# Loading the first input blocks of a blocked convolution by 121 lanes and by pairs of 50 lanes in place of 128

## The chip, the cores and the metric

The kernel runs on one core of one Trainium2 chip. The metric is the time of one execution on the device, in microseconds (us), as the median of several runs. TensorE (PE) multiplies matrices, VectorE (DVE), ScalarE (ACT) and GpSimd (POOL) do element-wise work, and the queue of SyncE (SP) issues the transfers, which run on the core's 16 DMA engines. A lane is one of the 128 partitions of the on-chip memory.

## The reference

Two steps: a long convolution along the sequence by FFT, and then a small expert layer on the 128 best-scored positions of each batch.

```python
# x: (8, 6336, 128), h: (6336, 128), float32
Xf = np.fft.rfft(x, n=2*S, axis=1); Hf = np.fft.rfft(h, n=2*S, axis=0)
y = np.fft.irfft(Xf * Hf[None], n=2*S, axis=1)[:, :S]
scores = y @ w_gate
for b in range(B):
    top = np.argpartition(-scores[b], 128)[:128]
    ye = np.maximum(y[b, top] @ w1, 0) @ w2
    y[b, top] += 1 / (1 + np.exp(-scores[b, top]))[:, None] * ye
```

## The kernel before

The transforms are written as products with tables of sines and cosines. The work is cut into units: unit -1 is the filter `h`, units 0 to 7 are the data. Each unit has eight input blocks. Block n belongs to unit n // 8 - 1, so blocks 0 to 7 are the filter, 8 to 15 are unit 0, and 16 onwards the later units. A block is a 128 x 1024 array of float32 in memory, 512 KB. On the host, 50 rows are put in lanes 0 to 49 and 50 rows in lanes 64 to 113; the other 28 lanes are zeros.

Stage A takes one block at a time. `load_x(n)` puts it into one of nine slots of the buffer `half`. `fold(n, v)` makes two passes of VectorE over it, a sum (L133) and a difference (L134). `products_a` then makes 2 x 16 TensorE products (L195, t = 0 and 1) with the lanes b*64 to b*64 + 49 alone, from the table `fah` for the filter and from `fa` for all data units, and `leave_a` copies them out of the accumulator by ScalarE (L212) and, from the fourth block of unit 0 on, in part by VectorE (L210). There are three accumulator places in turn.

The order is written out by hand in `plan`: stage A of unit -1, then stage A of unit 0, then steps "j", which join the filter's spectrum (`stage_h`, whose products stand at the helper's line L109) and unit 0's middle stage; then the stages of later units, interleaved. Blocks 0 to 8 are loaded ahead of all work. After the second half of block b of unit -1 (b = 0 to 6), the load of block b + 9 is issued on SP, into the slot that block b leaves. After block 3, behind the load of block 12, stand the loads of the constants `cst` and of the table `fa` (L848, L849). The folds are put on VectorE four blocks ahead of the products: ahead of the products of block b stands the fold of block b + 4, and the copies out of block b come behind it.

Each transfer that SP issues counts on one of eight semaphores in turn (DMAHW0 to DMAHW7 below), so a transfer waits until the one eight places ahead of it has landed.

Of the kernel before, what the change touches and what calls it, by code (L numbers as in the profile page):

```python
# [18 lines left out]
N1, N2 = 50, 128  # L19
# [5 lines left out]
LN = 114  # L25
# [8 lines left out]
def conv_moe(ctx, tc, x, h, w_gate, w1, w2, fa_d, wb_d, wc_d, at_d, tri_d, cst_d, outs):  # L34
    nc = tc.nc
# [75 lines left out]
    blocks = {}  # L111

    def place(n):
        u, q = n // 8 - 1, n % 8
        if u >= 2 and 0 < q < 5:
            o = 6400 + 1600 * (0, 1, 3, 2)[q - 1]
            return reg[u % 2][:, o:o + 1536]
        i = 10 + max(0, q - 4) % 3 if u >= 2 else (n + 3) % 9 if n < 16 else n - 13
        return half[:, i * 1536:i * 1536 + 1536] if i < 10 else xr[i - 10]

    def load_x(n):
        u, q = n // 8 - 1, n % 8
        t = place(n)
        for i in range(2 if n == 0 else 1):
            w = slice(i * 512, i * 512 + 512) if n == 0 else slice(0, 1024)
            nc.sync.dma_start(out=t[:, w], in_=h[q, :, w] if u < 0 else x[u, q])
        blocks[n] = (t[:, 0:1024].rearrange("p (d s m) -> p d s m", d=8, s=2),
                     t[:, 1024:1536].rearrange("p (d m) -> p d m", d=8))

    def fold(n, eng):  # L130
        for i in range(2 if n == 0 else 1):
            xs, es = [a[:, i * 4:i * 4 + 4] if n == 0 else a for a in blocks[n]]
            eng.tensor_tensor(out=es, in0=xs[:, :, 0], in1=xs[:, :, 1], op=ALU.add)  # L133
            eng.tensor_tensor(out=xs[:, :, 0], in0=xs[:, :, 0], in1=xs[:, :, 1], op=ALU.subtract)  # L134

# [608 lines left out]
    for u in range(NU):  # L744
        if u + 2 <= NU:
            both = merge(c_list(u), b_list(u + 1))
            n = next(i for i, s in enumerate(both) if s[0] == "b") + 2 * (u % 2)
# [56 lines left out]
    for n in range(9):  # L804
        load_x(n)
    v.memset(ones16, 1.0)
    v.memset(edges[:, 0:1], -1.0)
    v.memset(edges[:, 1:2], -0.5)
    fold(0, v)
    done = [1]  # L810

    def fold_to(n):
        while done[0] <= min(n, 23):
            fold(done[0], v if done[0] < 16 or done[0] in (20, 21, 23) else g)
            done[0] += 1
# [10 lines left out]
    for s in plan:  # L826
        kind, unit = s[0], s[1]
        n = (unit + 1) * 8
# [5 lines left out]
        if kind == "a":  # L834
            q, t = s[2:]
            if unit < 2 and t == 0:
                fold_to(min(n + q + 4, 15) if unit < 1 else 23)
            if unit >= 2 and (q, t) == (3, 0):
                fold(n + 7, g)
# [5 lines left out]
            if t and n + q < 7:  # L845
                load_x(n + q + 9)
# [5 lines left out]
            if unit >= 2 and (q, t) == (1, 0):  # L852
                load_x(n + 7)
            if t:
                visit("pqx" if q and q % 2 == 0 else "x")
        elif kind == "j":
# [4 lines left out]
            n = KCH[c][1] * HD  # L861
# [23 lines left out]
        elif kind == "c":  # L885
            stage_c(*s[1:])
            i = HALVES.index(s[2] // 2 * 2)
            free = True
            if unit + 2 < NU and s[2] % 2:
# [4 lines left out]
                q = (None, 0, None, None, 1, 4, 2, (3, 5))[i] if last else (None, 0, 5, 6, 1, 4, 2, 3)[i]  # L894
# [21 lines left out]
        elif kind == "d":  # L916
            busy[0] = unit + 1 == NU
            stage_d(*s[1:], tabs.pop(s))
            i = s[2]
# [129 lines left out]
```

## Time and profile before

| | |
|---|---|
| median of 3 runs | 785.18 us (784.46 to 789.2) |
| the profiled execution | 789.5 us, with a span of 787.7 us from first to last instruction |
| PE busy | 728.6 us, 92% of the span |
| DVE, ACT, POOL busy | 631.2, 449.4, 550.0 us |
| DMA | 157.64 MB, mean 200 GB/s |
| mean granted PE clock | 0.991 of full |

The page gives each engine's busy time, then the span in 40 slices of some 20 us. The change lies in the first two slices: stage A of the filter and of unit 0 runs from the start to 42.7 us. The profiled execution is 4.3 us longer than the median, and its span 1.8 us shorter than its own time.

### The profile page before, as it was taken

How to read it: one execution, taken by the hardware profiler on the slowest of the kernel's cores; microseconds unless marked ns; L12 is line 12 of the kernel's file. 1: busy time of each engine (PE TensorE's matmuls, PEld its weight loads, DVE VectorE, ACT ScalarE, POOL GpSimd, SP SyncE). 2: the span in 40 equal slices, each digit the busy share in tenths (PEclk: the TensorE clock that was granted, in tenths of full speed). 3: DMA queues.
4: the chain of work that ended last, by engine and by line, in shares of the span. 5: the costliest groups of instructions: out<-in, count | busy, mean ns of one | idle time of the engine just before them, and what ended most of it. 6: DMA issues, size and time to landing. Idle time of an engine off the chain costs nothing.

```text
span 787.7 us, 39722 instructions
## 1 busy us (share of the span) xinstructions
PE 728.6 (92%) x17566; PEld 630.3 (80%) x17566; DVE 631.2 (80%) x1072; ACT 449.4 (57%) x962; POOL 550.0 (70%) x405
## 2 busy tenths in 40 slices
PE   6899889999999999999999999999999998878665
PEld 5777678888889879888898789888897888868554
DVE  6579967767676799899777999999688998975983
ACT  5687643465346556656366466555564666665562
POOL 0029929976997599759968697877895756623733
PEclk9899999999999999999999999999999999999989
DMA  8539637567856775678557765699569736460500
GB/s 329 194 133 333 242 113 243 174 198 235 272 186 196 243 267 181 179 240 274 176 168 231 254 218 146 189 363 303 152 211 298 242 107 179 131 197 20 156 15 17
DMA packets 82292, 157.64 MB, mean 200 GB/s; under 512 B 9366, under 2 KB 30088, under 8 KB 82120
## 3 DMA queue, kind: packets, MB, share of 16 engines
q1 hardware_dynamic: 81224, 154.05, 61.0%
q8 instruction: 138, 2.26, 1.2%
q0 software_dynamic: 896, 1.05, 0.5%
q14 instruction: 34, 0.28, 0.1%
HBM read 121.77 MB, written 33.29 MB: 197 GB/s over the span
## 4 chain that ended last, share of the span: by engine, by line
PE 66%; DVE 17%; issue 5%; DMA 4%; POOL 3%; ACT 2%; SPq 1%; another core or an unknown queue 0%; POOLq 0%; DVEq 0%; ACTq 0%
PE pb L301 24%; PE pt L109 18%; PE pt L195 10%; PE pb L321 10%; DVE cmp L472 2%; DVE ss L353 2%; PE pb L195 2%; DVE tx L283 2%; PE pb L109 1%; POOL big L288 1%; DMA out<-st 1%; PE pm L109 1%; DVE st L330 1%; ACT junk L485 1%; DVE st L331 1%
## 5 line engine op out<-in xcount | busy, mean ns | idle before, releaser
L302 ACT COPY half<-pb 114x512 f32<-114x512 f32 x224 | 147.0, 656 | 166.8 <-PE pb L301 166.3
L288 POOL TENSOR_TENSOR big<-big,tx 128x512 f32<-128x512 f32 (+1 forms) x104 | 132.0, 1303 | 70.3 <-DVE tx L283 60.8
L337 POOL TENSOR_TENSOR tm<-st,wg 114x1024 f32<-114x1024 f32 x56 | 133.9, 2394 | 59.9 <-DVE st L331 41.3
L288 POOL TENSOR_TENSOR reg<-reg,tx 128x512 f32<-128x512 f32 (+1 forms) x104 | 130.8, 1291 | 44.3 <-PE pb L301 22.6
L301 PE MATMUL pb<-wc,reg 128*50 128x64 f32 x4096 | 125.6, 219 | 4.4 <-issue 3.7
L301 PEld LDWEIGHTS pb<-wc,reg 128*50 128x50 f32 x4096 | 120.4, 126 | 8.4 <-issue 5.2
L301 PEld LDWEIGHTS pb<-wc,big 128*50 128x50 f32 x4096 | 118.5, 126 | 4.1 <-issue 1.1
L301 PE MATMUL pb<-wc,big 128*50 128x64 f32 x4096 | 121.0, 219 | 0.8 <-issue 0.8
L321 PE MATMUL pb<-half,wbuf 114*50 114x128 f32 x1792 | 110.9, 273 | 2.9 <-issue 1.5
L321 PEld LDWEIGHTS pb<-half,wbuf 114*50 114x50 f32 x1792 | 96.5, 122 | 9.6 <-issue 2.5
L109 PE MATMUL pt<-big,wbuf 128*64 128x256 f32 x704 | 86.4, 388 | 0.5 <-issue 0.5
L109 PE MATMUL pt<-reg,wbuf 128*64 128x256 f32 x704 | 85.0, 388 | 0.0
L212 ACT COPY reg<-pt 128x800 f32<-128x800 f32 x66 | 58.0, 932 | 38.7 <-PE pt L195 37.2
L283 DVE TENSOR_TENSOR tx<-pt,wbuf 128x1024 f32<-128x1024 f32 (+1 forms) x65 | 76.3, 1174 | 0.0
L330 DVE TENSOR_TENSOR st<-pb,st 114x512 f32<-114x512 f32 x56 | 38.6, 689 | 42.1 <-PE pb L321 27.1
L109 PEld LDWEIGHTS pt<-big,wbuf 128*64 128x64 f32 x704 | 52.1, 135 | 23.7 <-issue 1.0
L109 PEld LDWEIGHTS pt<-reg,wbuf 128*64 128x64 f32 x704 | 51.7, 135 | 21.4
L355 DVE TENSOR_REDUCE ss<-tm 114x16 f32<-114x1024 f32 x48 | 58.4, 1216 | 7.5 <-POOL tm L337 6.9
L212 ACT COPY big<-pt 128x800 f32<-128x800 f32 x56 | 49.2, 938 | 24.3 <-PE pt L195 24.3
L283 DVE TENSOR_TENSOR reg<-pt,wbuf 128x1024 f32<-128x1024 f32 (+1 forms) x39 | 45.9, 1178 | 17.9 <-PE pt L109 17.8
L195 PE MATMUL pt<-fa,big 50*64 50x100 f32 x2336 | 59.2, 249 | 0.3 <-issue 0.3
L195 PEld LDWEIGHTS pt<-fa,big 50*64 50x64 f32 x2336 | 51.9, 133 | 6.5 <-issue 3.6
(177 smaller groups left out, 1193.8 us busy)
## 6 DMA issues: line engine op xcount, KB each, us to landing
wbuf<-tab_at SPq DMA_DIRECT2D x112, 200.0 KB
out<-st SPq DMA_DIRECT2D x112, 200.0 KB
wbuf<-tab_wb SPq DMA_DIRECT2D x84, 256.0 KB
wbuf<-hd SPq DMA_DIRECT2D x84, 256.0 KB
big<-in_x SPq DMA_DIRECT2D x37, 512.0 KB
half<-in_x SPq DMA_DIRECT2D x15, 512.0 KB
hd<-st SPq DMA_DIRECT2D x24, 256.0 KB
reg<-in_x SPq DMA_DIRECT2D x12, 512.0 KB
```

The source lines that it names most:

```text
L109: nc.tensor.matmul(out[lo:hi], w[:, lo:hi], r, **k)
L195: nc.tensor.matmul(o, w, tab[lanes, c], start=True, stop=True)
L212: nc.scalar.copy(out=o, in_=i)
L283: v.tensor_tensor(out=dst.rearrange("p h a j k t -> p k h a j t"), in0=src, in1=w, op=ALU.mult)
L288: g.tensor_tensor(out=yv[:, :, r], in0=yv[:, :, r], in1=zv[:, :, 1 - r], op=ALU.add if r else ALU.subtract)
L301: nc.tensor.matmul(pt[i2 * 64:i2 * 64 + N1, o:o + HD], w, wc[:, i2], start=True, stop=True)
L302: nc.scalar.copy(out=hv[0:LN, c * 4 + j:c * 4 + j + 2].rearrange("p j r m t -> p (j r) t m"), in_=pt[0:LN].rearrange("p (j t m) -> p j t m ...
L321: nc.tensor.matmul(pt[r][a * 64:a * 64 + N1, c * 128:c * 128 + 128], ats[c // 2][0:LN, c % 2, a, r], hv[0:LN, :, r, m], start=True, stop=True)
L330: v.tensor_tensor(out=st[:, 0:512], in0=pt[1][0:LN], in1=st[:, 512:1024], op=ALU.add)
L337: (v if split else g).tensor_tensor(out=tm.rearrange("p (a d) -> p a d", d=n), in0=st.rearrange("p (a d) -> p a d", d=n), in1=w.unsqueeze( ...
L353: v.tensor_reduce(out=ss[u][:, 0, :, 4 * i + k:4 * i + 4], in_=tv[:, :, k:4], axis=AX.X, op=ALU.add)
L355: v.tensor_reduce(out=ss[u][:, :, :, 4 * i:4 * i + 4].rearrange("p b s c -> p s c b"), in_=tm.rearrange("p (s c b d) -> p s c b d", s=2, c ...
```

## The change

Blocks 1 to 8 are loaded by one transfer of lanes 0 to 120 in place of 0 to 127. Blocks 9 to 15 are loaded by two transfers each, of lanes 0 to 49 and of lanes 64 to 113. The folds of all blocks, those of the later units too, work on lanes 0 to 113 in place of 0 to 127. Block 0 and blocks 16 onwards are loaded as they were.

```diff
     def load_x(n):
         u, q = n // 8 - 1, n % 8
         t = place(n)
-        for i in range(2 if n == 0 else 1):
+        for i in range(2 if n == 0 or 8 < n < 16 else 1):
             w = slice(i * 512, i * 512 + 512) if n == 0 else slice(0, 1024)
-            nc.sync.dma_start(out=t[:, w], in_=h[q, :, w] if u < 0 else x[u, q])
+            p = slice(i * 64, i * 64 + N1) if 8 < n < 16 else slice(0, 121 if 0 < n < 9 else 128)
+            nc.sync.dma_start(out=t[p, w], in_=h[q, p, w] if u < 0 else x[u, q, p])
...
     def fold(n, eng):
         for i in range(2 if n == 0 else 1):
-            xs, es = [a[:, i * 4:i * 4 + 4] if n == 0 else a for a in blocks[n]]
+            xs, es = [a[0:LN, i * 4:i * 4 + 4] if n == 0 else a[0:LN] for a in blocks[n]]
```

N1 is 50 and LN is 114. The order of the work is the same; SP's queue gets seven more transfers. Before, the queue from block 8 to block 13 reads as follows (line, transfer with its lanes and elements, semaphores waited for):

```order
L126 DMA half<-in_x 128x1024 [waits DMAHW2_49]
L126 DMA half<-in_x 128x1024 [waits DMAHW3_49,DVE_49,PE_49]
L126 DMA half<-in_x 128x1024 [waits DMAHW4_49,DVE_49,PE_49]
L126 DMA half<-in_x 128x1024 [waits DMAHW5_49,DVE_49,PE_49]
L126 DMA half<-in_x 128x1024 [waits DMAHW6_49,DVE_49,PE_49]
L848 DMA cst<-tab_cst 128x14 [waits DMAHW7_49]
L849 DMA fa<-tab_fa 128x200 [waits DMAHW0_49]
L126 DMA half<-in_x 128x1024 [waits DMAHW1_49,DVE_49,PE_49]
```

After, the same stretch of SP's queue, from block 8 to the first half of block 13:

```order
L127 DMA half<-in_x 121x1024 [waits DMAHW2_49]
L127 DMA half<-in_x 50x1024 [waits DMAHW3_49,DVE_49,PE_49]
L127 DMA half<-in_x 50x1024 [waits DMAHW4_49,PE_49]
L127 DMA half<-in_x 50x1024 [waits DMAHW5_49,DVE_49,PE_49]
L127 DMA half<-in_x 50x1024 [waits DMAHW6_49,PE_49]
L127 DMA half<-in_x 50x1024 [waits DMAHW7_49,DVE_49,PE_49]
L127 DMA half<-in_x 50x1024 [waits DMAHW0_49,PE_49]
L127 DMA half<-in_x 50x1024 [waits DMAHW1_49,DVE_49,PE_49]
L127 DMA half<-in_x 50x1024 [waits DMAHW2_49,PE_49]
L849 DMA cst<-tab_cst 128x14 [waits DMAHW3_49]
L850 DMA fa<-tab_fa 128x200 [waits DMAHW4_49]
L127 DMA half<-in_x 50x1024 [waits DMAHW5_49,DVE_49,PE_49]
```

The table `fa` still stands behind block 12, but there are four more transfers ahead of it, and its semaphore is now that of the second half of block 9 in place of block 6.

## Rows read from the trace of the kernel before

**Rows 1.** The page: busy time of each engine, and the chain's shares by engine.
```profile
PE 728.6 (92%) x17566; PEld 630.3 (80%) x17566; DVE 631.2 (80%) x1072; ACT 449.4 (57%) x962; POOL 550.0 (70%) x405
PE 66%; DVE 17%; issue 5%; DMA 4%; POOL 3%; ACT 2%; SPq 1%; another core or an unknown queue 0%; POOLq 0%; DVEq 0%; ACTq 0%
```
**Rows 2.** Timeline, PE: start, us, group, [idle before, and its end].
```profile
15.37 0.99 PE L195 MATMUL pt<-half 50*64 50x100 f32 x35 [0.52 <-issue]
21.29 0.44 PE L195 MATMUL pt<-half 50*64 50x100 f32 x4 [2.84 <-issue]
27.53 0.25 PE L195 MATMUL pt<-fa,half 50*64 50x100 f32 x1
34.54 0.48 PE L195 MATMUL pt<-fa,half 50*64 50x100 f32 x11 [1.61 <-issue]
38.06 0.48 PE L195 MATMUL pb<-fa,half 50*64 50x100 f32 x12 [0.56 <-issue]
...
42.71 2.94 PE L109 MATMUL pb<-reg,wbuf 128*64 128x256 f32 x24
```
**Rows 3.** DMA queues (packets, MB, share of 16 engines) in 15.4:18.7 and 18.7:19.9.
```profile
q1 hardware_dynamic: 369, 1.36, 102.9%
...
q1 hardware_dynamic: 140, 0.47, 99.8%
q8 instruction: 1, 0.02, 5.7%
```
**Rows 4.** The same in 34.6:35.6 and 35.6:36.6.
```profile
q1 hardware_dynamic: 3, 0.00, 1.2%
...
q8 instruction: 1, 0.02, 5.8%
```
**Rows 5.** Windows: stretch, busy us (x) of PE, PEld, DVE, ACT, POOL; clock, DMA share, GB/s.
```profile
9.00:13.00 4.00, 3.86 (x86) 3.56 (x89) 3.90 (x7) 1.60 (x4) 0.00 (x0) 1.00 1.03 422
...
16.00:17.00 1.00, 1.00 (x58) 1.00 (x52) 0.96 (x3) 1.00 (x2) 0.00 (x0) 1.00 1.03 410
...
22.00:23.00 1.00, 1.00 (x32) 1.00 (x28) 0.90 (x3) 0.85 (x1) 0.00 (x0) 0.50 0.63 242
23.00:24.00 1.00, 1.00 (x32) 1.00 (x28) 0.90 (x2) 0.75 (x2) 0.00 (x0) 0.50 0.02 8
...
26.00:27.00 1.00, 1.00 (x35) 1.00 (x31) 0.20 (x1) 0.85 (x1) 0.00 (x0) 0.53 0.35 66
```
**Rows 6.** Timeline, SP's issues.
```profile
6.46 10.38 SPq L126 DMA_DIRECT2D half<-in_x  x5
...
17.38 0.42 SPq L849 DMA_DIRECT2D fa<-tab_fa  x1
17.91 8.38 SPq L126 DMA_DIRECT2D half<-in_x  x3
```
**Rows 7.** Timeline, DVE: the folds of blocks 1 and 14, and a copy.
```profile
7.97 0.69 DVE L133 TENSOR_TENSOR half<-half 128x512 f32<-128x512 f32 x1 [2.13 <-DMA half<-in_h]
...
26.80 0.69 DVE L133 TENSOR_TENSOR half<-half 128x512 f32<-128x512 f32 x1 [1.11 <-DMA half<-in_x]
...
39.38 0.99 DVE L210 COPY big<-pt 128x800 f32<-128x800 f32 x1
```
**Rows 8.** Windows late in the span, where only 50-lane stores of results are queued.
```profile
728.00:728.60 0.60, 0.60 (x16) 0.60 (x13) 0.33 (x1) 0.00 (x0) 0.49 (x1) 1.00 0.65 160
...
734.00:737.00 3.00, 2.16 (x48) 1.92 (x44) 2.96 (x8) 1.32 (x6) 2.93 (x2) 1.00 0.59 201
```
**Rows 9.** Lines L126 and L358 of SP: issues, ns min/median/max, first and last start.
```profile
L126 SPq DMA_DIRECT2D half<-in_x x13: 327/365/720, 6.5 to 68.5; - x13
...
L358 SPq DMA_DIRECT2D out<-reg x16: 777/787/922, 726.0 to 746.0; - x16
```
**Rows 10.** The page, costliest groups: a DVE pass over 114 lanes.
```profile
L330 DVE TENSOR_TENSOR st<-pb,st 114x512 f32<-114x512 f32 x56 | 38.6, 689 | 42.1 <-PE pb L321 27.1
```
**Rows 11.** Late in the span: PE's longest idle time there, and the clock.
```profile
750.45 0.21 PE L109 MATMUL pm<-num,ones 114*64 114x7 bf16 x2 [7.95 <-DVE num L474]
...
747.00:754.00 7.00, 3.56 (x36) 3.25 (x36) 6.17 (x24) 4.51 (x19) 2.21 (x4) 0.51 0.16 53
```

## The prediction

> **What bounds the kernel now.** I read the page first. PE is busy for 92% of the span and holds 66% of the chain of waits [rows 1], so what lengthens or shortens PE's work in some stage moves the end by as much. The change lies in stage A of the first sixteen blocks, so I read that stretch next, in the timeline of PE. Stage A ends when the first product of the filter's join starts, at 42.71 us, and unit 0's first product, the first to read the table fa, stands at 27.53 [rows 2]. So unit -1 takes 27.5 us and unit 0 takes 15.2 us. In these stretches PE has idle times that end with nothing that a semaphore shows ("issue"): 0.52, 2.84, 1.61 and 0.56 us, 5.5 us in all [rows 2].
>
> The view of the DMA queues tells what they are. In 15.4:18.7, right after PE resumed at 15.37, no packet of the instruction queue (q8) is there, and the data queue keeps all 16 engines busy at 103%; one 16 KB packet of q8 falls in 18.7:19.9, and PE resumes at 21.29 [rows 2, 3]. When PE resumes at 34.54 the DMA engines are idle (1.2%), and the next packet of q8 starts in the stretch that begins 1.1 us later [rows 2, 4]. So PE's code comes in over the same engines; it starts about 1.1 us after it is asked for in quiet and about 3.3 us in the flood of input blocks. The 2.84 us idle time is that flood's. It has a second price: the granted clock goes to half, and PE then starts 32 matmuls in a microsecond in place of 58 [rows 5].
>
> **The change part by part.** The transfers come first. In the flood 16 engines move 422 GB/s, 26.4 each, so a 512 KB block takes 1.24 us [rows 5]. How many engines a transfer of 121 lanes takes, the trace doesn't show. It shows that the 50-lane stores keep a share of 0.59 to 0.65 of the 16 busy, that is about 10 engines, at 160 to 201 GB/s in sum, 16 to 20 each [rows 8]. Sixteen for 128 lanes and ten for 50 are both the largest number up to 16 that divides the lanes; by that pattern 121 lanes take 11. [...]
>
> So blocks 1 to 8 (121 lanes, 496 KB in thousands) cost between 496/(11 x 26.4) = 1.71 us, if each engine keeps the flood's pace, and 496/(11 x 16.0) = 2.82 us, if it falls to that of the slowest stores. A pair of 50 lanes (410 KB) costs between 410/264 = 1.55 us and 410/160 = 2.56 us. The direction speaks for the flood's row (loads, as here), the shape for the stores' rows (50 lanes of the same places, in pairs). I take the middle between the flood's row and the better store row, 20.1 GB/s an engine: 1.71 and 2.24 give 1.98 us for 121 lanes; 1.55 and 2.04 give 1.80 us for a pair.
>
> [...]
>
> Who waits for the slower stream? Folds do, block by block, but PE has slack there: before, block 1's fold waited for its bytes until 7.97 [rows 7] and the next ones came every 1.24 us, while PE, with its stalls and its half clock, came to block 8 only at 27.53. The waiter that matters is the table fa. Its issue stands behind block 12's [rows 6], so its bytes come when those of blocks 0 to 12 have passed. Before, the stream runs dry between 22 and 23 us (share 0.63, then 0.02) [rows 5], that is at 22.6, with block 13 behind fa; so fa was there at about 22.6 - 1.24 + 0.5 (from last byte to waiter: block 14's bytes end at about 26.35, by the share of 0.35 in 26:27, and its fold begins at 26.80 [rows 5, 7]) = 21.9, and hid behind PE's lag by 5.6 us. With the change, blocks 1 to 8 add 8 x (1.98 - 1.24) = 5.9 us and blocks 9 to 12 add 4 x (1.80 - 1.24) = 2.2 us: fa is there at 30.0, and the cover is gone. PE reaches it well before: unit -1's blocks now come in every 1.98 us, block 7's by about 7.97 + 7 x 1.98 = 21.8, and its products are done some 3 us later. So unit 0 starts at 30.1 in place of 27.53: **+2.6 us**.
>
> From there to the end of stage A it was 15.2 us before, with the idle times 1.61 and 0.56 in it [rows 2]. PE now waits with its next code already loaded, and the fetch that came late before finds engines that the pairs leave free; I take the 1.61 as gone and keep the 0.56, which stood in quiet: **-1.6 us**. The idle time before fa is some 5 us long. The clock went to half after 2.84 us of it here and after 7.95 us late in the span, and not after 1.61 [rows 2, 5, 11]; so I expect it at half again. It came back 5.7 us after PE resumed at 21.29, and 3.5 us after 750.45. At 32 starts in place of 58 in a microsecond that costs 0.45 us in each, 1.6 to 2.6 us, of which some would be waits for code or copies anyway: **+1.5 us**.
>
> The rest hides. Block 15's bytes pass at 30.0 + 0.4 + 3 x 1.80 = 35.8; its fold ends at 37.4, and VectorE's six copies of blocks 11 to 15 behind it (at most 0.99 each [rows 7], under 6 us) end before 43.4, about with PE. If the stream were much slower than taken, this would be late next. The seven added issues cost SP 0.37 us each by the median of the loads or 0.79 by that of the stores [rows 9], 2.6 to 5.5 us; four blocks are queued ahead of the engines at any time, so SP waits for landings and not the engines for SP. The folds on 114 lanes cost nothing and gain nothing: a pass over 114 x 512 takes 689 ns [rows 10] and one over 128 x 512 takes 690 [rows 7]. After stage A all else stands as it was, and moves by the same shift.
>
> The sum is 2.6 - 1.6 + 1.5 = **+2.5 us**. The profiled execution's span would go from 787.7 to 790.2; the median of the runs, 785.18, to 787.7, which I round to **788 us**. One per cent, 7.9 us, is about what a measurement of this kernel tells from no change.
>
> **The rivals.** First, *the code comes in on an engine that stays free, and the loads keep the flood's pace* (1.71 and 1.55). For it: 26.4 GB/s is the only load row; against: the store rows. Blocks 1 to 12 then add only 8 x 0.47 + 4 x 0.31 = 5.0 us, fa is there at 26.9, 0.6 before 27.53; the 1.61 us goes, and the clock may stay up: -2.2, and with the other idle times shortened as well some -3 to -4: 781 to 783. It can't be more, since block 15 then still lands at 32 and its fold and six copies follow. Second, *the fewer engines get in each other's way*, and each falls to 16.0 GB/s: 8 x (2.82 - 1.24) + 4 x (2.56 - 1.24) = 17.9 us more, fa at 39.8, unit 0 from 39.9: +12.4 - 1.6 + 1.5 = +12.3, 797 us, slower by 1.6%. For it: the rate of 160 in the first store row; against: 201 in the longer one. It turns slower by over 1% when fa comes after about 35.4, which is an engine's rate below some 18.5 GB/s. Third, *121 lanes still spread over all 16 engines*, since the trace has no such transfer: then only blocks 9 to 12 are late, by 2.2 us, fa comes at 24.1, hidden, and the fetches wait as before: 784 to 785.
>
> **How the numbers follow.** The forecast's middle rates have a chance of 0.50, the fast rival 0.27, the slow one 0.18, the third 0.05. The two ends of the range are the two rivals' ends: 781 to 797. Faster by over 1% needs more than stage A can give by any of these sums: 0.03. Slower by over 1% is the slow rival: 0.18. The rest, 0.79, is within 1%.
>
> **What would show it.** In the profile after: DMA's share in the first 25 us at about 11/16 = 0.69 in place of 1.03; the timeline of PE with a wait for the DMA of fa before unit 0's first product, at about 30; the 2.84 us idle time gone or covered by that wait; the granted clock at half once, near 25 to 35 us; the first product of the join at about 45. The forecast is wrong if fa has no wait (the stream is faster), if VectorE's folds wait 2.5 us and more between blocks (the second rival), or if the stretches behind stage A don't keep their length.

## The result, and the profile after

The changed kernel takes 792.15 us (median of 6 runs, 790.85 to 796.81), the kernel before on the same chip 784.66 (6 runs, 783.83 to 789.2): a ratio of 1.0089, with an interval of 1.0062 to 1.0117. It is slower by 0.9%, some 7 us. (The ratio and its interval are worked out from all runs; the two medians by themselves are 7.5 us apart.) The profiled execution took 791.53 us, with a span of 789.8.

The page of the changed kernel, busy time and the chain by engine, beside [rows 1]:

```profile
PE 730.8 (93%) x17566; PEld 638.2 (81%) x17566; DVE 630.2 (80%) x1072; ACT 449.8 (57%) x962; POOL 549.8 (70%) x405
...
PE 70%; DVE 14%; DMA 6%; issue 5%; ACT 2%; POOL 2%; SPq 0%; POOLq 0%; DVEq 0%; ACTq 0%
```

PE has the same 17566 products and 2.2 us more busy time. DMA's share of the chain goes from 4% to 6%. The timeline of PE in stage A (start, us, group, idle before and its end), beside [rows 2]:

```profile
25.82 0.50 PE L196 MATMUL pb<-half 50*64 50x100 f32 x9 [3.07 <-issue]
29.48 1.73 PE L196 MATMUL pt<-fa,half 50*64 50x100 f32 x32 [1.82 <-DMA fa<-tab_fa]
...
39.11 0.48 PE L196 MATMUL pt<-fa,half 50*64 50x100 f32 x11 [1.53 <-issue]
...
42.91 0.48 PE L196 MATMUL pb<-fa,half 50*64 50x100 f32 x12 [0.83 <-issue]
...
47.55 1.80 PE L109 MATMUL pb<-reg,wbuf 128*64 128x256 f32 x14
```

Unit 0's first product starts at 29.48 in place of 27.53, after a wait for the table fa; the join starts at 47.55 in place of 42.71, 4.84 us later. The row with 4 products, which the wait of 2.84 us stood ahead of, has no wait of its own any more; the 3.07 us stand some 126 products later, with nine products of unit -1 and then one group of 32 still to come. The row with 11 products stands at the same place of the program before and after. From unit 0's start to it, without the idle time ahead of it, PE took 34.54 - 1.61 - 27.53 = 5.40 us before and takes 39.11 - 1.53 - 29.48 = 8.10 now, for the same products.

The windows tell why (stretch, busy us of the engines, clock, DMA share, GB/s), beside [rows 5]:

```profile
9.00:13.00 4.00, 2.84 (x58) 2.54 (x62) 2.77 (x4) 1.38 (x3) 0.00 (x0) 1.00 0.72 265
13.00:17.00 4.00, 4.00 (x132) 4.00 (x128) 3.14 (x5) 2.94 (x6) 0.00 (x0) 1.00 0.73 282
...
21.00:25.00 4.00, 1.76 (x74) 1.57 (x67) 2.78 (x5) 2.52 (x5) 0.00 (x0) 1.00 0.65 240
25.00:29.00 4.00, 1.83 (x41) 1.52 (x40) 3.23 (x5) 1.81 (x3) 0.00 (x0) 0.63 0.69 244
29.00:33.00 4.00, 3.52 (x83) 3.55 (x86) 2.77 (x4) 1.36 (x3) 0.00 (x0) 0.50 0.85 242
33.00:37.00 4.00, 4.00 (x124) 4.00 (x120) 2.06 (x3) 2.77 (x6) 0.00 (x0) 0.59 1.00 280
```

DMA's share is 0.72 while the 121-lane blocks pass and 0.65 for the pairs, which fits 11 and 10 engines of 16; the sum falls from 422 GB/s to 265 to 282 and to 240. The granted clock falls to half about when PE starts again after the first idle time (0.63 in 25:29) and stays there while unit 0 begins (0.50 in 29:33), in place of being back at full by 27 us.

VectorE's folds, the sums of blocks 1, 7, 8 and 12, beside [rows 7]:

```profile
9.28 0.69 DVE L134 TENSOR_TENSOR half<-half 114x512 f32<-114x512 f32 x1 [2.82 <-DMA half<-in_h]
...
20.05 0.69 DVE L134 TENSOR_TENSOR half<-half 114x512 f32<-114x512 f32 x1 [0.24 <-DMA half<-in_h]
22.33 0.69 DVE L134 TENSOR_TENSOR half<-half 114x512 f32<-114x512 f32 x1 [0.87 <-DMA half<-in_x]
...
29.09 0.69 DVE L134 TENSOR_TENSOR half<-half 114x512 f32<-114x512 f32 x1 [0.20 <-DMA half<-in_x]
```

Blocks 1 to 7 come every (20.05 - 9.28)/6 = 1.80 us, block 8 another 2.28 us behind, and the pairs of blocks 9 to 12, behind block 8's at 22.33, every (29.09 - 22.33)/4 = 1.69. A pass still takes 0.69 us. SP's queue, beside [rows 6]:

```profile
6.32 16.34 SPq L127 DMA_DIRECT2D half<-in_x  x9
...
23.86 0.75 SPq L850 DMA_DIRECT2D fa<-tab_fa  x1
```

The table is issued at 23.86 in place of 17.38 and is waited for until 29.48. A page of PE's code (queue q8) still comes in amid the loads: the DMA queues in 23.2:24.4, beside [rows 3, 4]:

```profile
q1 hardware_dynamic: 132, 0.29, 62.4%
q8 instruction: 1, 0.02, 5.3%
```

That packet of q8 stands in the idle time that ends at 25.82, though only 62% of the engines' time is taken by data.

How far the lateness goes is seen at the same two instructions late in the span. VectorE's timeline of the kernel before:

```profile
687.97 0.06 DVE L423 MEMSET bb<- 114x1 f32 x1
...
736.90 0.94 DVE L353 TENSOR_REDUCE ss<-reg 114x6 f32<-114x768 f32 x1
```

and of the kernel after:

```profile
694.30 0.06 DVE L424 MEMSET bb<- 114x1 f32 x1
...
737.46 0.94 DVE L354 TENSOR_REDUCE ss<-reg 114x6 f32<-114x768 f32 x1
```

The first is 6.33 us later: 4.84 from stage A and 1.5 from between. The second is 0.56 us later, so 5.77 us come back between the two, and the profiled spans differ by 2.1 us only. Between the two instructions, PE of the kernel before waits in 695:735 as follows (us in total, times, longest):

```profile
PE pb L301 <- issue: 3.2, 8, 0.5
```

The trace after has no such row. The profiled execution of before was one of its long ones (789.5 against a median of 784.66), and these waits are 3.2 of the 5.77 us; where the rest comes from isn't shown. The waits aren't the change's: the first eight kernels below, whose kernel before took 791 or 792 us, have six to eight of them (2.4 to 3.3 us in total), and the last four, whose kernel before took 784, have none.

### The profile page after: what moved, and what is told of

Its sections match the earlier page's. It is cut to its first block, busy times and chain, and to the rows that moved or that the text cites. A ratio compares the mean times of both kernels' runs of the same rounds, so it can differ in the third digit from the quotient of the medians.

```text
span 789.8 us, 39741 instructions
## 1 busy us (share of the span) xinstructions
PE 730.8 (93%) x17566; PEld 638.2 (81%) x17566; DVE 630.2 (80%) x1072; ACT 449.8 (57%) x962; POOL 549.8 (70%) x405
## 4 chain that ended last, share of the span: by engine, by line
PE 70%; DVE 14%; DMA 6%; issue 5%; ACT 2%; POOL 2%; SPq 0%; POOLq 0%; DVEq 0%; ACTq 0%
PE pb L302 25%; PE pt L109 20%; PE pb L322 10%; PE pt L196 9%; PE pb L109 3%; DVE cmp L473 2%; PE pm L109 2%; DMA half<-in_x 2%; POOL tm L338 2%; ACT junk L486 1%; DVE ss L354 1%; DMA wbuf<-tab_wb 1%; DMA half<-in_h 1%; DVE st L331 1%; DVE tx L284 1%
## 5 line engine op out<-in xcount | busy, mean ns | idle before, releaser
L302 PE MATMUL pb<-wc,reg 128*50 128x64 f32 x4096 | 124.0, 219 | 2.2 <-ACT st L326 1.9
L109 PEld LDWEIGHTS pt<-big,wbuf 128*64 128x64 f32 x704 | 56.4, 135 | 20.3 <-issue 1.4
L284 DVE TENSOR_TENSOR reg<-pt,wbuf 128x1024 f32<-128x1024 f32 (+1 forms) x39 | 45.9, 1177 | 18.7 <-PE pt L109 18.7
```

The source lines that it names most:

```text
L109: nc.tensor.matmul(out[lo:hi], w[:, lo:hi], r, **k)
L284: v.tensor_tensor(out=dst.rearrange("p h a j k t -> p k h a j t"), in0=src, in1=w, op=ALU.mult)
L302: nc.tensor.matmul(pt[i2 * 64:i2 * 64 + N1, o:o + HD], w, wc[:, i2], start=True, stop=True)
```

## The experiments

Three theories stand behind the expectations. **Table**: unit 0 waits for fa, and that is what costs (the prediction's step). **Code**: PE's code pages come late beside the loads, and the clock falls in the idle time; that costs wherever the table stands. **Hindering**: transfers that aren't cut over 128 lanes slow each other on the engines (the prediction's second rival). Each ratio is to the kernel before, run beside it on the same chip.

**The folds alone.** Transfers as before.

```diff
-            xs, es = [a[:, i * 4:i * 4 + 4] if n == 0 else a for a in blocks[n]]
+            xs, es = [a[0:LN, i * 4:i * 4 + 4] if n == 0 else a[0:LN] for a in blocks[n]]
```

> The folds work on 114 lanes; all transfers are as before. Both theories, that of the table (fa comes late behind a slower stream) and that of the code (PE's code comes late behind the pairs), expect no change: ratio to before 0.999 to 1.001, stage A's end at 42.7 us within 0.5. If the folds on fewer lanes cost something themselves, the ratio is 1.003 or more.

Measured: 1.0014 (0.9988 to 1.0040), join at 43.55, which is 0.84 later where 0.5 was allowed. The folds' lanes cost nothing that can be told in the time, and the windows show the old flood (415 GB/s in 9:13).

**Blocks 1 to 8 by 121 lanes, 9 to 15 by 128.** From the changed kernel:

```diff
-        for i in range(2 if n == 0 or 8 < n < 16 else 1):
+        for i in range(2 if n == 0 else 1):
...
-            p = slice(i * 64, i * 64 + N1) if 8 < n < 16 else slice(0, 121 if 0 < n < 9 else 128)
+            p = slice(0, 121 if 0 < n < 9 else 128)
```

> Blocks 1 to 8 by 121 lanes and folds on 114; blocks 9 to 15 by 128 lanes as before. The table: blocks 1 to 8 at the 1.80 us of the changed kernel add 8 x 0.56 = 4.5 us, fa comes at about 26.4, before unit 0 needs it at 27.5, so the ratio is 0.998 to 1.002 and no wait for fa stands. The code: the first two fetches run beside 11 engines and are early, the pairs are gone, so the 3.07 us idle time is gone or shorter than 2 us and the time is at or below before: ratio 0.995 to 1.001. A third reading, that any slower stream costs by itself: 1.004 or more.

Measured: 1.0080 (1.0048 to 1.0112), unit 0 at 31.42, join at 48.27. Its windows:

```profile
9.00:13.00 4.00, 3.78 (x76) 3.17 (x75) 2.75 (x5) 1.91 (x4) 0.00 (x0) 1.00 0.91 280
...
17.00:21.00 4.00, 2.71 (x95) 2.11 (x88) 1.78 (x3) 3.08 (x5) 0.00 (x0) 1.00 1.00 242
```

Here all 16 engines are busy (1.00) and move less (242 GB/s, 15 each) than 11 of them did above (265 to 282, 24 to 26 each). This is what the hindering theory says, here with transfers of both cuts queued together. There is no wait for fa, and the ratio lies above all that the table and code theories allow (1.002): such a loss needs no wait for fa.

**Blocks 9 to 15 by pairs, 1 to 8 by 128 lanes.** From the changed kernel:

```diff
-            p = slice(i * 64, i * 64 + N1) if 8 < n < 16 else slice(0, 121 if 0 < n < 9 else 128)
+            p = slice(i * 64, i * 64 + N1) if 8 < n < 16 else slice(0, 128)
```

> Blocks 9 to 15 by pairs of 50 lanes and folds on 114; blocks 1 to 8 by 128 lanes as before. The table: only blocks 9 to 12 are slower, 4 x 0.45 = 1.8 us, fa comes at about 24 and is hidden: ratio 0.999 to 1.002. The code: fetches in 20 to 30 us wait behind the pairs on ten engines as in the changed kernel, so idle times of 3 us and more stay, the clock goes to half, and most of the loss stays: ratio 1.004 to 1.009.

Measured: 1.0034 (1.0004 to 1.0065), unit 0 at 27.82, join at 47.13. PE's timeline:

```profile
26.37 0.41 PE L196 MATMUL pb<-half 50*64 50x100 f32 x9 [3.95 <-issue]
...
34.14 2.09 PE L196 MATMUL pt<-fa,half 50*64 50x100 f32 x42 [3.15 <-issue]
...
47.13 2.94 PE L109 MATMUL pb<-reg,wbuf 128*64 128x256 f32 x24
```

Unit 0 starts on time, with no wait for the table, and the join is nearly as late as after the whole change (47.55). The table can't be the cause alone. What stands there is two waits for code, 3.95 and 3.15 us. The ratio lies between the two theories' ranges (up to 1.002, and from 1.004).

**The table early.** The changed kernel with fa loaded right behind block 3:

```diff
+        if n == 3:
+            nc.sync.dma_start(out=fa, in_=fa_d[:, 0])
...
-                nc.sync.dma_start(out=fa, in_=fa_d[:, 0])
```

> The changed kernel with the load of fa issued behind block 3's, ahead of blocks 4 to 8. The table: the 1.82 us wait for fa goes, and with it some of the half clock: 2 to 4 us less than the changed kernel, ratio to before 1.004 to 1.006. The code: the idle times of 3.07 and 1.53 us stay, and at most the 1.82 us go, less if the code is what comes late next: ratio 1.006 to 1.009.

Measured: 1.0053 (1.0026 to 1.0080), unit 0 at 27.19, join at 48.04. PE's timeline:

```profile
26.28 0.41 PE L196 MATMUL pb<-half 50*64 50x100 f32 x9 [2.06 <-issue]
32.14 1.16 PE L196 MATMUL pt<-fa,half 50*64 50x100 f32 x42 [1.27 <-issue]
38.49 0.77 PE L196 MATMUL pt<-fa,half 50*64 50x100 f32 x11 [3.26 <-issue]
48.04 2.26 PE L109 MATMUL pb<-reg,wbuf 128*64 128x256 f32 x18
```

The wait for fa is gone and unit 0 starts 2.3 us sooner than after the change; the join is no sooner (47.55 there). The waits for code are what is late next: 2.06, 1.27 and 3.26 us. But the ratio is what the table theory expected (1.004 to 1.006) and less than the code theory did (1.006 to 1.009): 4.2 us lost, in place of 7.0 and, in the run once more below, 8.5. The joins of single traces don't contradict that, since the stream of this one was slower (214 GB/s in 9:13 and 245 in 13:17, for 265 and 282). The intervals overlap, so what fa's wait is worth, from nothing to some 4 us, stays open; it isn't the whole loss, since the two experiments above lose 6.3 and 2.7 us without it.

**Six slots in place of nine**, so that fewer blocks are queued ahead, once on the kernel before and once on the changed one:

```diff
-        i = 10 + max(0, q - 4) % 3 if u >= 2 else (n + 3) % 9 if n < 16 else n - 13
+        i = 10 + max(0, q - 4) % 3 if u >= 2 else (n + 3) % 6 if n < 16 else n - 13
...
-    for n in range(9):
+    for n in range(6):
...
-            if t and n + q < 7:
-                load_x(n + q + 9)
+            if t and n + q < 10:
+                load_x(n + q + 6)
```

> The kernel before with six slots for the first 16 blocks in place of nine: block n + 6 is loaded when block n is done, so fewer loads stand queued at a time. The code (PE's code waits behind what is queued): the 2.84 us idle time shrinks to under 1.5, unit 0 and the join come earlier by 2 us or more (join at 38 to 41 us), ratio 0.994 to 0.998. The table: fa was hidden and stays so, ratio 0.999 to 1.001. Against both: the loads are asked for too late, folds wait for bytes, the join comes at 43 or later, ratio 1.001 or more.

> The changed kernel with six slots in the same way; fa then stands behind block 9. The code: with less queued, the idle times of 3.07 and 1.53 us shrink, join at 43 to 45.5 in place of 47.55, ratio to before 1.001 to 1.005. The table: fa comes some 5 us earlier, its wait of 1.82 goes and nothing more, join at about 45.7, ratio 1.006. If the stream's own pace is what binds, the join stays at 47 or later.

Measured: 1.0006 (0.9983 to 1.0030) on the kernel before, with the join at 43.94, and 1.0114 (1.0077 to 1.0150) on the changed one, with the join at 50.48. On the kernel before, PE's timeline has the long wait for code shorter:

```profile
19.97 0.43 PE L195 MATMUL pt<-half 50*64 50x100 f32 x4 [2.02 <-issue]
28.43 1.16 PE L195 MATMUL pt<-fa,half 50*64 50x100 f32 x42 [0.88 <-issue]
33.16 0.48 PE L195 MATMUL pt<-fa,half 50*64 50x100 f32 x11 [1.63 <-issue]
39.30 0.48 PE L195 MATMUL pb<-fa,half 50*64 50x100 f32 x12 [1.52 <-issue]
```

2.02 for the 2.84 of [rows 2], and 1.52 for the 0.56; the four add up to 6.05 us, with one of 0.23 at 14.87 to 6.28, and the waits for code in [rows 2] to 5.53. There is no gain in sum. On the changed kernel the wait ahead of the last nine products of unit -1 is 3.77 us, longer than with nine slots. A queue of six blocks is no remedy, as the code theory expected it to be.

**Blocks 1 to 15 by 120 lanes**, a number that 15 divides. From the changed kernel, `range(2 if n == 0 else 1)` and:

```diff
-            p = slice(i * 64, i * 64 + N1) if 8 < n < 16 else slice(0, 121 if 0 < n < 9 else 128)
+            p = slice(0, 120 if 0 < n < 16 else 128)
```

> Blocks 1 to 15 by one transfer of 120 lanes, which divides by 15. If each engine keeps its pace (26.4 GB/s), the share is 0.94 and a block takes 1.24 us as with 128 lanes: join at 42 to 44, ratio 0.998 to 1.002. If engines hinder each other at the memory's side when a transfer isn't cut as one of 128 lanes is, the share stays high and the rate falls: 1.8 us a block or more, under 300 GB/s, join at 45 or later, ratio 1.003 or more.

Measured: 1.0097 (1.0063 to 1.0130), unit 0 at 37.89, join at 55.28. Its windows:

```profile
12.00:16.00 4.00, 4.00 (x104) 4.00 (x100) 2.56 (x5) 2.49 (x4) 0.00 (x0) 1.00 0.97 236
```

Fifteen engines are busy and move 236 GB/s, 15.7 each, where the flood's sixteen moved 26.4 each [rows 5], with nothing of another cut between the blocks. So it isn't the mixing alone, and fifteen engines in place of eleven don't help.

**Five slots**, on the kernel before (as with six, with 5 for 6 and 11 for 10).

> The kernel before with five slots: fewer loads queued still. The code: idle times that end with no semaphore shrink further than with six, but the time from issue to landing, 2.8 us at best, is no longer covered and folds wait: join at 38 to 43. If the queue's length has nothing to do with the late code, the 2.84 us idle time stands as before and the join comes later than with six.

Measured: 1.0043 (1.0017 to 1.0069), join at 47.41. PE's timeline:

```profile
24.81 0.65 PE L195 MATMUL pb<-half 50*64 50x100 f32 x9 [2.72 <-issue]
...
41.25 1.43 PE L195 MATMUL pb<-fa,half 50*64 50x100 f32 x26 [4.81 <-DVE big L210]
```

At the place of the 2.84 the wait is 0.63 us (at 18.95), and one of 2.72 stands some 126 products later. These two are all the waits for code, 3.35 us in place of 5.53, so fewer blocks in the queue may make them shorter after all; but a new wait of 4.81 us for a copy behind late folds takes over, and may hide others. Fewer slots cost more than they give.

**The changed kernel once more**, word for word.

> The changed kernel once more, word for word, to tell what of its 7.5 us comes again. Stage A ended at 47.55 us in place of 42.71 in its first trace, 4.8 later, and some 2 us more arose between 146 and 218 us. Code theory (only stage A's stalls and its half clock are the change's): 4 to 6 us slower than the kernel before, ratio 1.005 to 1.008, join between 46.5 and 48.5, and the 2 us behind it need not come again. Table theory and hindering theory say nothing else of this kernel. If the ratio is 1.009 or more with the join near 47.5, something behind stage A belongs to the change too.

Measured: 1.0109 (1.0080 to 1.0138), 792.77 us against 783.93. All the expectations of its trace missed. Windows:

```profile
9.00:13.00 4.00, 3.71 (x79) 3.16 (x76) 2.36 (x4) 1.82 (x3) 0.00 (x0) 1.00 0.73 187
13.00:17.00 4.00, 4.00 (x118) 3.95 (x116) 1.71 (x3) 2.87 (x5) 0.00 (x0) 1.00 0.70 185
...
21.00:25.00 4.00, 3.26 (x100) 2.90 (x100) 1.63 (x3) 1.71 (x3) 0.00 (x0) 0.77 0.70 184
...
29.00:33.00 4.00, 1.46 (x36) 1.15 (x28) 2.51 (x5) 1.80 (x3) 0.00 (x0) 0.50 0.69 240
```

PE's timeline of the same trace:

```profile
28.47 0.66 PE L196 MATMUL pb<-half 50*64 50x100 f32 x9 [0.98 <-issue]
36.00 1.73 PE L196 MATMUL pt<-fa,half 50*64 50x100 f32 x31 [5.54 <-DMA fa<-tab_fa]
45.18 0.48 PE L196 MATMUL pt<-fa,half 50*64 50x100 f32 x11 [2.12 <-issue]
48.71 0.49 PE L196 MATMUL pb<-fa,half 50*64 50x100 f32 x12 [0.56 <-issue]
...
53.62 2.94 PE L109 MATMUL pb<-reg,wbuf 128*64 128x256 f32 x24
```

VectorE's timeline of it, two folds and the late instruction:

```profile
16.67 0.69 DVE L134 TENSOR_TENSOR half<-half 114x512 f32<-114x512 f32 x1 [1.27 <-DMA half<-in_h]
19.37 0.69 DVE L134 TENSOR_TENSOR half<-half 114x512 f32<-114x512 f32 x1 [1.28 <-DMA half<-in_h]
...
695.40 0.06 DVE L424 MEMSET bb<- 114x1 f32 x1
```

The same kernel, the same eleven engines (share 0.70 to 0.73), and 185 GB/s in place of 265 to 282: a 121-lane block every 2.70 us in place of 1.80. The chip doesn't explain that alone: the kernel with all blocks by 121 lanes (below), on the same chip as this trace, moved 225 to 279, and the one with the table early went from 214 to 275 within one execution. Unit 0 waits for fa until 36.00 and the join comes at 53.62, 6.07 us later than in the first trace. Late in the span the two are only 1.1 us apart (695.40 and 694.30). One step of the 5 us that come back between can be seen: near 100 us, PE of the first trace has three waits for code (0.70, 1.20 and 0.82 us) in unit 1's products that the second has not, and the kernel before has (0.75, 0.93 and 0.82). So the stream has no one rate for this cut, and one trace couldn't tell.

**Blocks 1 to 15 by 112 lanes and 2 lanes**, so that sixteen engines take nearly all of it:

```diff
-        for i in range(2 if n == 0 or 8 < n < 16 else 1):
+        for i in range(2 if n < 16 else 1):
...
-            p = slice(i * 64, i * 64 + N1) if 8 < n < 16 else slice(0, 121 if 0 < n < 9 else 128)
+            p = slice(i * 112, 112 + i * 2) if 0 < n < 16 else slice(0, 128)
```

> Blocks 1 to 15 by two transfers, of 112 and of 2 lanes. Hindering theory in the form that only transfers cut as the kernel before cuts them (16 engines, all in step) keep 26 GB/s an engine: 112 lanes go over 16 engines with 7 lanes each, but the two lanes behind each block set engines out of step, so rates of 240 to 280 GB/s, folds every 1.7 to 2 us, join at 47 to 50, ratio 1.005 to 1.010. Rival: sixteen engines are what gives the rate, whatever the lanes: share 1.0 and 400 GB/s or more, folds every 1.2 to 1.33 us as before, join 42 to 44, ratio 0.998 to 1.002.

Measured: 1.0064 (1.0044 to 1.0084), join at 47.75. Windows:

```profile
9.00:13.00 4.00, 3.87 (x82) 3.56 (x86) 2.75 (x5) 1.84 (x4) 0.00 (x0) 1.00 1.03 240
13.00:17.00 4.00, 3.23 (x130) 3.12 (x126) 2.72 (x5) 2.88 (x5) 0.00 (x0) 1.00 1.02 252
```

Sixteen engines, as full as in the flood (1.03), at 240 to 252 GB/s: 15 to 16 each. The rival (sixteen engines give the rate, whatever the lanes) is out. That the two lanes behind each block are what slows the 112 isn't tested by itself; the 120 lanes above, with nothing behind them, were as slow.

**Blocks 1 to 15 all by 121 lanes.** From the changed kernel, `range(2 if n == 0 else 1)` and:

```diff
-            p = slice(i * 64, i * 64 + N1) if 8 < n < 16 else slice(0, 121 if 0 < n < 9 else 128)
+            p = slice(0, 121 if 0 < n < 16 else 128)
```

> Blocks 1 to 15 all by 121 lanes in one transfer. Hindering theory (what hinders is the mixing of cuts, as in the kernel with 121 and 128 lanes, where blocks came every 1.9 to 2.8 us): without mixing the blocks come every 1.80 us to the end, share 0.70, 270 to 280 GB/s, fa between 27 and 30. Code theory: five engines stay free for code all through, so a code page starts in the stream's time 1.1 to 2 us after it is asked for in place of 2.8, and the join comes at 44 to 47, ratio 1.002 to 1.006. Rival: the engine that brings a page is one of the eleven as often as not, join at 47 to 49, ratio 1.006 to 1.010.

Measured: 1.0138 (1.0106 to 1.0171), the highest ratio of all, beyond each expectation. Unit 0 waits 5.87 us for fa, until 33.55, and the join comes at 52.84. The rate rose from 225 GB/s (9:13) to 279 (25:29) and fell to 243, at a share of 0.85, when the tables `wbuf` were queued behind the blocks (29:33). Engines that stay free for code didn't pay.

**Blocks 1 to 15 by two halves**, lanes 0 to 63 and 64 to 127. From the changed kernel, `range(2 if n < 16 else 1)` and:

```diff
-            p = slice(i * 64, i * 64 + N1) if 8 < n < 16 else slice(0, 121 if 0 < n < 9 else 128)
+            p = slice(i * 64, i * 64 + 64) if 0 < n < 16 else slice(0, 128)
```

> Blocks 1 to 15 by two transfers of 64 lanes each, lanes 0 to 63 and 64 to 127, with the bytes of the kernel before. It tells whether the number of engines or the half of the lanes sets the pairs' rate of 234 to 250 GB/s. If sixteen engines in step are what counts: 16 engines, 400 GB/s or more, folds every 1.24 to 1.33 us, join 42 to 44, ratio 0.998 to 1.003. If a transfer into one half of the lanes is held to that half: share 1.0 at 220 to 280 GB/s, folds every 1.9 to 2.3 us, join at 50 or later, ratio 1.008 to 1.015.

Measured: 1.0114 (1.0082 to 1.0145), join at 53.68. Windows:

```profile
9.00:13.00 4.00, 3.72 (x78) 3.42 (x82) 2.64 (x5) 1.60 (x4) 0.00 (x0) 1.00 1.03 248
13.00:17.00 4.00, 2.75 (x85) 2.64 (x79) 2.52 (x5) 2.65 (x4) 0.00 (x0) 1.00 1.04 251
```

The same bytes as before, all 128 lanes, sixteen engines, and 248 GB/s in place of 422 because the block is cut in two. That fits the expectation's second case, a transfer held to its half, but the 112 lanes, which reach into both halves, ran no faster (240 to 252 GB/s); the half alone doesn't explain it.

The join's lateness in the trace (against 42.71) and what each kernel lost in time (the ratio's part above one, times the median of before beside it):

| kernel | blocks 1 to 8; 9 to 15, lanes | join, us later | time, us more |
|---|---|---|---|
| folds alone | 128; 128 | 0.8 | 1.1 |
| six slots | 128; 128 | 1.2 | 0.5 |
| five slots | 128; 128 | 4.7 | 3.4 |
| pairs alone | 128; pairs | 4.4 | 2.7 |
| 121 alone | 121; 128 | 5.6 | 6.3 |
| the change | 121; pairs | 4.8 | 7.0 |
| the change again | 121; pairs | 10.9 | 8.5 |
| table early | 121; pairs | 5.3 | 4.2 |
| change, six slots | 121; pairs | 7.8 | 9.0 |
| 112 and 2 | 112 and 2 | 5.0 | 5.0 |
| all 121 | 121; 121 | 10.1 | 10.8 |
| two halves | 64 and 64 | 11.0 | 8.9 |
| 120 lanes | 120; 120 | 12.6 | 7.7 |

In sum the joins are 84 us later and the times 75 us longer: some nine tenths of what stage A loses reach the end. Each kernel's join is one execution's, and its time that of six or more, which is part of the scatter: line by line the two differ by up to 5 us. Every cut other than one transfer of 128 lanes loses 2.7 us or more, and none gains.

## Why the prediction was right, and where its steps were not

The time came out within the range and within 1%, 4 us above the forecast. Against the kernel before beside it the loss is 7.0 us (8.5 in the second comparison), where +2.5 was forecast. That it stayed within 1% is in part luck: the second comparison, 1.0109, is beyond it, and the intervals of both reach over it. By its own steps:

- **The engines.** 11 for 121 lanes and 10 for 50: shares of 0.72 and 0.65. Right. By the same pattern 120 lanes took 15 (0.97), and 112 and 64 took 16 (1.03). The third rival is out.
- **The rates.** 1.98 us was taken for a block of 121 lanes and 1.80 for a pair; the first trace has 1.80 and 1.69, the second 2.70 for the block. The middle rate lies between the two executions and describes neither: the 121-lane blocks ran near the first rival's end (24 to 26 GB/s an engine; it took 26.4) in one and near the second's (16.8; it took 16.0) in the other, while the pairs ran at 24 in both. The second rival put the border of 1% at a table that comes after about 35.4; in the second trace unit 0 waits for it until 36.00.
- **The wait for fa, +2.6.** It is there, as forecast, with +1.95 (29.48) in the first trace and +8.5 (36.00) in the second. The mechanism was right. But it isn't the whole loss: blocks of 120 lanes, of 112 and 2 and of two halves lose 5.0 to 8.9 us with no wait for fa, and with the table early 4.2 us stay.
- **The idle time for code gone, -1.6.** This term failed. The prediction put it that PE "now waits with its next code already loaded" and that the late fetch "finds engines that the pairs leave free". The 1.61 us is now 1.53 (2.12 in the second trace). The 2.84 is gone at its place, as forecast, but a wait of 3.07 stands some 126 products later, where there was none: PE stops for code ahead of the last nine products of unit -1, and then again for the table. Free engines didn't bring the code as in quiet: from PE's start at 25.82 to the next packet of q8 it took 2.9 us, and with no loads queued it takes 1.1 (39.11 to 40.22; before, 34.54 to 35.65). In the old flood it took 3.4 (15.37 to 18.81), and the wait behind it, ahead of the row with 4 products, 2.84 us. The wait at that place is longer behind blocks of 112 and 2 lanes (5.31, until 24.32), of 120 (4.03, until 27.76) and of two halves (4.40, until 27.12). So the slower stream, which also lasts longer, can keep the code waiting as well as the table; the prediction had the pairs free the way for it.
- **The half clock, +1.5.** Right in kind and mis-sized. Unit 0's first products take 8.10 us in place of 5.40 at half clock, +2.7. The prediction priced 3.5 to 5.7 us at half; it lasted some 7 us of unit 0 (0.50 in 29:33, 0.59 in 33:37), where two idle times, 3.07 and 1.82, stand one behind the other. In the second trace unit 0's part is 7.06 us, +1.7, and the clock fell already in 21:25 (0.77), ahead of both long idle times, after a stretch in which PE was busy for 2.93 of 4 us (17:21); why it fell there isn't shown.
- **Together, unit 0's part.** Forecast -0.1, measured 18.07 - 15.18 = +2.9 us: +2.7 for the clock, -0.1 for the idle time of 1.53, +0.3 for the later ones. With fa's +1.95 that is the 4.84 of the trace. In the second trace unit 0's part is +2.4 and fa +8.5.
- **What hides.** The folds' lanes cost nothing (1.0014), as forecast. SP's seven added issues held nothing up that the trace shows, apart from the transfers that stand behind them.
- **Behind stage A all moves by the same shift.** Nearly: +1.5 more in the first trace, -3.5 in the second, and nine tenths over all kernels. The 7.0 us of the first comparison are 4.8 of stage A and such a rest; where each step of that rest comes from stays open but for the one shown near 100 us.

So the direction was right and the size was not: the sum had one term that didn't come (code, -1.6 forecast, +0.2 measured) and one too small (clock, +1.5 forecast, +2.7 measured), and took the rest of the program to add nothing (2.2 us in the first comparison). How slow the stream is differs from execution to execution, which no sum from the trace before could tell; the result lies within the range because the range took in both ends.

Of how the engines slow each other only the rates are shown. At 112 lanes, 120 lanes and two halves, 15 or 16 busy engines share 236 to 252 GB/s, and one uncut transfer of 128 lanes after another gives 422. The cause was not shown: the trace doesn't tell which lanes an engine writes, and whether the engines meet there or at the memory that they read was not tried. Nor is it shown why the changed kernel had two rates (265 to 282 and 185 GB/s) on one and the same cut.

Pairs moved 240 GB/s and the two halves 248 to 251, both with transfers of the other half queued beside them; what one half takes by itself was not tried. What the last experiment shows is that two transfers of the halves don't add up to one over all lanes (422).

## What to carry to other kernels

Cutting unneeded lanes off a transfer saved bytes here and cost more than the bytes: a block of 121 lanes came every 1.80 us, and every 2.70 in the second trace, where one of 128 took 1.24. Look at the rate with other cuts in the trace of the kernel itself, since blocks cut into 112 and 2 of 128 lanes ran at 0.6 of the whole's rate here (240 to 252 GB/s for 422). Where several things are late by about the same amount (a table, a page of code, the clock), taking one away can give less than its size (the table's wait of 1.82 us went with the table early, and the join came at 48.04, no sooner than 47.55); ask for each idle time what ends next. And a rate read from one execution of a new transfer shape is one draw: a second profile of the same kernel showed some two thirds of it (185 GB/s for 265 to 282).

## What the runs showed of the hardware

The same kernel's load stream ran at 265 to 282 GB/s in one execution and at 185 in another, with the same share of busy engines (0.70 to 0.73). Sixteen busy engines moved anything from 240 to 422 GB/s, by how the block was cut (112 and 2 lanes, and 128). Waits for PE's code pages of 16 KB took 0.2 to 5.3 us each in stage A (5.31 with 112 and 2 lanes), also with engines free of data (3.07 us at a share of 0.62). After such a wait the next page's packet started 1.1 us behind PE's start where no loads were queued, 3.4 us behind it in the flood of uncut blocks, and 2.9 us behind it beside the pairs (25.82 to 28.67). And six to eight waits of up to 0.5 us in one group of products late in the span, 2.4 to 3.3 us in total, are in some executions and not in others, with and without the change.
